# Seven more second exponential parts on VectorE, later passes for them, and feed-forward tiles issued ahead of due passes at one step in four

## The chip, the cores and the metric

The kernel runs on one core of one Trainium2 chip. The metric is the time of one execution on the device in microseconds (us), the median of several runs. The profiler's record of one execution gives every instruction's start and duration.

## The reference, cut to what matters

One transformer block over 2048 tokens with 512 features: layer norm, attention with 32 heads of 16 features, residual; layer norm, a gated feed-forward layer of width 1792, residual.

```python
scores = einsum("bhqd,bhkd->bhqk", q, k) * (Dh ** -0.5)     # 32 heads, 2048 x 2048
p = softmax(scores, axis=-1)
o = einsum("bhqk,bhkd->bhqd", p, v)
h = x + o_as_rows @ wo
g, u = ln(h) @ w_gate, ln(h) @ w_up                          # 512 -> 1792
out = h + (sigmoid(g) * u) @ w_down                          # 1792 -> 512
```

There are 32 x 2048 x 2048 exponentials, 1,048,576 on each of 128 partitions.

## The kernel before, in words

**Steps and cycles.** The exponentials are cut into units of 128 keys x 512 (head, query) columns. Three units make a *step*; there are 683 steps (0 to 682). Four steps make a *cycle*; "place 0" to "place 3" is the step's number modulo 4. A cycle is named here by its first step. In each step `emit_scores` writes the score matmuls of three units (L951) into one of two PSUM tiles `pss` (step number modulo 2), and ScalarE takes the exponential of all three in one instruction (L964, 128x1536). So the scores of step i+2 need the reads of step i's tile to be over.

**Parts on VectorE.** In the steps of the set `split`, ScalarE takes only two units (128x1024) and VectorE computes the third one's exponential by bit arithmetic: `exp_bits` (L989, reads PSUM) at once, and then three *passes*, `exp_first` (L992 and L995) one step later, `exp_second` (L998) two steps later and `exp_third` (L1002, writes the unit) three steps later. They are put into a table of due calls, `due`, by `later`. Place 0 of every cycle from step 8 to 672 has such a part (484 and 540 excepted). Some cycles have a second part at place 2; these steps form the set `twice`. There are 15 from two loops (226, 242, 258, 274, ..., 402, 418, 434, 458, 470) and three given by number (522, 638, 646). In the cycles of `twice` all scores are written as pairs of half-height matmuls, and otherwise those of odd steps only.

**PV.** The product with V (`emit_pv`, L1056) of a cycle's twelve units is three calls, planned by `plan_pv`. All three stand at step n+6 for the cycle that starts at n, those that begin a new group of heads one step later. The accumulator `acc` is one PSUM bank, which `emit_norm` copies out (L1020) at a group's end. The third call reads the unit of a second part: the unit of step n+2 computed on VectorE is the first one of it.

**Filler.** Everything else is a generator, `filler`, that is drawn on step by step through `emit_fill`. From step 185 on it is the output projection and the feed-forward layer of the chunk of queries before the one at work. There are eight chunks: 512, 512, 256, 256 and four of 128 queries. Chunk by chunk it gives the output projection (`ffn_wo` for chunks 0 and 1, `ffn_wo_tight` for the rest: matmuls L650, then addition L662, statistics L149 and the scaling L160 on VectorE, and transposes L166), gate and up (`ffn_up`), and down (`down_tile`, L706 and L711). In `ffn_up` a gate tile (matmuls L687, then tanh on ScalarE, L693) is written at place 3 and an up tile (matmuls L687, then the multiplication on VectorE, L703) at place 1. All these tiles share one PSUM bank, `pm`, so the next tile's matmuls wait until the last one is read. In `ffn_wo` the first half of a projection tile is at place 3 and the second half, with L662 and L149, at place 1. `state["rate"]` is 8.0 while such a chunk's work is issued and None otherwise.

**Order.** Every engine's instructions are issued in the order in which the program calls them. In each step that order is: scores, exponential and bits of step i; PV; the due passes; the filler. Before the change the filler went ahead of the due passes only for a tile that ends in a transpose or a last down part (`state["turn"]`), and ahead of a PV call that begins a new group:

```python
            us = pv_due.pop(i, [])
            early_fill = i >= 2 * CYC and any(u[2] == 0 for u in us)
            for u in us:
                if early_fill and u[2] == 0:
                    emit_fill(i)
                emit_pv(*u[:3], i)
            if state["turn"] and i == state["wait"] and not early_fill:
                emit_fill(i)
                early_fill = True
            for fn in due.pop(i, []):
                fn()
            if 1 <= i < NS and not early_fill:
                emit_fill(i)
```

Of the kernel before, what the change touches and what calls it, by code (L numbers as in the profile page):

```python
# [20 lines left out]
def kernel(  # L21
# [28 lines left out]
    CYC = 4  # L50
# [460 lines left out]
    def first_step(c):  # L511
        return NS * CHUNKS[c][0] / S if c < NC else NS
# [400 lines left out]
    def calm(i):  # L913
        filled = rate(i) and state["wait"] <= i and not state["done"]
        return not filled and not n_pv.get(i, 0)

    def emit_scores(i):
        group = groups[i]
        n = len(group)
        pss = pss2[i % 2]  # L920
        idle = i >= 3 * FIRST and (state["done"] or state["wait"] > i + CYC)
        pairs = i < FIRST and (i < 35 or i % CYC in (1, 2)) or i >= FIRST and (i % 2 == 1 or i - i % CYC + 2 in twice) and not idle
        still = i and calm(i) and calm(i + 1) and i - 1 not in split
        pairs = pairs and not still
        made[i] += 2 if pairs else 3
        if i % CYC == 0 and made[i - 1] <= 3 and i - 1 not in split and not pairs:
            g, s, _, _, j0, _ = part_of(group[0][0], *group[0][2:])
            m = per_bank(group[0][1])
            nc.tensor.matmul(pss[:, 0, :], lhsT=KT[:, g, 0:P], rhs=q_cols(group[0][0], s, j0 if m == 1 else 0, m),
                             start=True, stop=True)  # L930
            made[i] += 1
        order = [(ui, qg, part_of(qg, k, j)) for ui, (qg, c, k, j) in enumerate(group)]
        if pairs and order[0][2][4] // 2 == order[1][2][4] // 2:
            order[1:] = order[:0:-1]
        parts = [u + (a,) for a in range(2) for u in order[:2]] + [u + (a,) for u in order[2:] for a in range(2)]
        if i < OB:
            for ui, (_, c, k, j) in enumerate(group):
                nc.tensor.matmul(pss[:, ui, :], lhsT=KT[:, 0, k * P:(k + 1) * P], rhs=QB[1][:, j, :],
                                 start=True, stop=False)
            for ui, (_, c, k, j) in enumerate(group):  # L940
                nc.tensor.matmul(pss[:, ui, :], lhsT=ident_bf[:, j:j + 1].to_broadcast([P, P]), rhs=bnd[:],
                                 start=False, stop=True)
            parts = []
        for ui, qg, (g, s, kt, nk, j0, nh), a in parts:
            if a >= nk:
                continue
            assert ("k", g // 2) in ready
            h0 = 64 * (j0 // 2)
            rows = slice(h0, h0 + 64) if pairs else slice(0, P)
            o = QC // nk  # L950
            nc.tensor.matmul(pss[:, ui, a * o:(a + 1) * o], lhsT=KT[rows, g, (kt + a) * P:(kt + a + 1) * P],  # L951
                             rhs=q_cols(qg, s, j0, nh, rows), start=True, stop=True,
                             tile_position=(h0, 0) if pairs else None)
        for qg, c, k, j in group:
            if j == 3 and qg + 1 < len(qgs):
                k0 = 12 if per_bank(c) == 1 else 0
                if k == k0:
                    emit_q_rows(qg + 1)
                if k == k0 + (2 if k0 == 0 else 0):
                    emit_q_bound(qg + 1)  # L960
        slot = i % 7
        pt = pt4[slot] if slot < 4 else (pt_early if i < GM else pt_late)[slot - 4]
        na = n - 1 if i in split else n
        ex = nc.scalar.activation(out=pt[:, 0:na, :], in_=pss[:, 0:na, :], func=ACT.Exp, scale=DH ** -0.5 / QS)  # L964
        if na < n:
            scratch = scratch_of(i)
            src, dst = pss[:, na, :], pt[:, na, :]
            if len(scratch[0].shape) == 3:
                src, dst = (v.rearrange("p (a b) -> p a b", a=4) for v in (src, dst))
            tc.declare_no_dep(exp_bits(src, *scratch).ins, ex.ins,  # L970
                              reason="both only read, from different banks")
            later(i + 1, lambda: exp_first(*scratch))
            later(i + 2, lambda: exp_second(*scratch))
            later(i + 3, lambda: exp_third(dst, *scratch))
        for ui, u in enumerate(group):
            p_of[u] = pt[:, ui, :]

# [13 lines left out]
    def exp_first(e_bits, e_man, e_pol):  # L991
        nc.vector.tensor_scalar(out=e_man, in0=e_bits, scalar1=0x7FFFFF, scalar2=-0x40800000,  # L992
                                op0=ALU.bitwise_and, op1=ALU.bitwise_or)
        m = e_man.bitcast(FP32)
        nc.vector.scalar_tensor_tensor(out=e_pol, in0=m, scalar=PA, in1=m, op0=ALU.add, op1=ALU.mult)  # L995

    def exp_second(e_bits, e_man, e_pol):
        nc.vector.scalar_tensor_tensor(out=e_pol, in0=e_pol, scalar=PB, in1=e_man.bitcast(FP32),  # L998
                                       op0=ALU.add, op1=ALU.mult)

    def exp_third(dst, e_bits, e_man, e_pol):
        nc.vector.scalar_tensor_tensor(out=dst, in0=e_pol, scalar=PC, in1=e_bits.bitcast(FP32),  # L1002
                                       op0=ALU.add, op1=ALU.mult)
# [61 lines left out]
    def later(i, fn):  # L1065
        due.setdefault(i, []).append(fn)
# [3 lines left out]
    state = {"turn": False, "wait": 0, "debt": 0.0, "done": False, "next": 0, "rate": None}  # L1070
# [51 lines left out]
    twice = set()  # L1122
    for n0, n1 in ((223, 357), (393, 476)):
        for n in range(n0, n1):
            if n % ((4 if n < n0 + 56 else 3) * CYC) == 0 and n != 448:
                twice.add(n + 2)
    twice |= {522, 638, 646}
    split |= twice
    split -= {484, 540}

    def plan_pv():
        plan, last = {}, 0
        for n, group in enumerate(groups):
            if n < G1:
                if n % CYC == 0:
                    last = n + CYC + 2
                    for k, u in enumerate(units[n * GU:(n + CYC) * GU:4]):
                        if k and u[2] == 0:
                            last += 1
                        plan.setdefault(last, []).append(u)  # L1140
            else:
                for u in group:
                    if u[3] == 3:
                        last = max(last, n + LAG)
                        plan.setdefault(last, []).append(u)
        return plan

    with tc.manual_schedule():
        p1ctx = ExitStack()
        pmh["pool"] = p1ctx.enter_context(tc.tile_pool(name="ps_p1", bufs=6, space=PSUM))  # L1150
        prologue(p1ctx.enter_context(tc.tile_pool(name="pro", bufs=1)))
        p1ctx.close()
        pmh["pool"] = ps_misc
        sctx = ExitStack()
        ps_s = sctx.enter_context(tc.tile_pool(name="ps_s", bufs=1, space=PSUM))
        ptp = sctx.enter_context(tc.tile_pool(name="ptp", bufs=1))
        pss2 = [ps_s.tile([P, GU, QC], FP32, name=f"pss{k}") for k in range(2)]
        pt4 = [ptp.tile([P, GU, QC], BF16, name=f"pt{k}") for k in range(4)]
        later(12, clear_wo)
        later(72, load_wo)  # L1160
        later(90, lambda: nc.gpsimd.tensor_copy(out=ident_f[:], in_=ident_bf[:]))
        load_w()
        pv_due = plan_pv()
        n_pv = {i: len(us) if i < G1 + CYC else 0 for i, us in pv_due.items()}
        for i in range(NS + LAG):
            if i < NS:
                emit_scores(i)
            if i == NS + LAG - 1:
                while next(fl, None) == 1:
                    pass  # L1170
# [3 lines that stand above are left out]
                if early_fill and u[2] == 0:  # L1174
                    emit_fill(i)
                emit_pv(*u[:3], i)
            if state["turn"] and i == state["wait"] and not early_fill:
                emit_fill(i)
                early_fill = True
            for fn in due.pop(i, []):  # L1180
# [3 lines that stand above are left out]
        for _ in fl:  # L1184
            pass
        sctx.close()
        pmh["pool"] = ctx.enter_context(tc.tile_pool(name="ps_t", bufs=6, space=PSUM))
        pmh["work"] = ctx.enter_context(tc.tile_pool(name="tail", bufs=4))
        assert not due
        ffn_last(NC - 1)  # L1190
# [30 lines left out]
```

## Time and profile before

| | |
|---|---|
| median of 3 runs | 938.57 us (938.12 to 938.9) |
| profiled execution: its time, its span | 937.02 us, 935.2 us |
| granted TensorE clock in it | 1.000 |
| exponentials on ScalarE | first 28.6 us, last ends 915.0 us after the span's start |
| busy: ScalarE (ACT), TensorE matmul (PE), VectorE (DVE) | 896.8, 843.0, 760.6 us |
| gate and up multiplications (L703, width 512) | 54 |
| parts on VectorE (bits, L989) | 183 |

Durations are those of one profiled execution. A row of the timeline gives start, duration, engine, line, operation, tiles written and read, count, and in brackets the engine's idle time ahead of it with what ended it. Starts of instructions that follow each other on an engine can lie closer together than the duration of one, since the end of one overlaps with the start of the next. Times are from the span's start.

### The profile page before, as it was taken

To read this page: it belongs to the slowest core of one execution; us is meant where nothing else is said; L and a number is where in the kernel's file an instruction comes from. 1 tells how busy PE (TensorE), PEld (TensorE's weight loads), DVE (VectorE), ACT (ScalarE), POOL (GpSimd) and SP (SyncE) were. 2 spreads that over 40 slices of the span, in tenths; PEclk is the share of its full clock that TensorE was granted. 3 is DMA by queue.
4 is the path that set the end of the run, shared out by engine and by line. 5 is a ranking of instruction groups with operands and counts; after the bars stand their busy time and mean duration, and the time that the engine had idled before them with its cause. 6 is when DMAs were issued, how large, how long until landed. Compare 5 with 4: busy or idle time off the path is not lost.

```text
span 935.2 us, 21055 instructions
## 1 busy us (share of the span) xinstructions
PE 843.0 (90%) x8328; PEld 370.9 (40%) x8328; DVE 760.6 (81%) x1400; ACT 896.8 (96%) x778; POOL 32.5 (3%) x52
## 2 busy tenths in 40 slices
PE   5998888888889999998889999999999999998897
PEld 2322222222223232222233333333555675766575
DVE  8589988888788888898888888888778777778853
ACT  6999999999999999999999999999999999999992
POOL 5300000000000000000000000000000000000000
PEclk9999999999999999999999999999999999999999
DMA  5202350000003000001001100001000101100000
GB/s 165 47 2 68 118 131 16 16 16 11 10 24 106 16 16 16 7 21 28 15 22 27 32 10 16 16 26 33 16 12 26 23 11 22 27 24 17 18 24 14
DMA packets 43599, 29.48 MB, mean 32 GB/s; under 512 B 22764, under 2 KB 39852, under 8 KB 43500
## 3 DMA queue, kind: packets, MB, share of 16 engines
q1 hardware_dynamic: 43356, 28.01, 11.6%
q8 instruction: 65, 1.06, 0.5%
q14 instruction: 34, 0.28, 0.1%
q10 hardware_dynamic: 144, 0.13, 0.0%
HBM read 20.05 MB, written 2.36 MB: 24 GB/s over the span
## 4 chain that ended last, share of the span: by engine, by line
PE 46%; ACT 31%; DVE 15%; issue 5%; DMA 1%; POOL 0%; SPq 0%; ACTq 0%; DVEq 0%; POOLq 0%
PE pss L951 23%; ACT pt L964 17%; PE acc L1056 8%; PE pm L687 6%; ACT stg L964 6%; ACT wd L964 4%; ACT QTu L964 3%; PE pm L706 2%; DVE stg L989 2%; PE pm L650 2%; DVE st L149 1%; PE pm L175 1%; DVE pt L1002 1%; DVE reg L992 1%; DVE y L998 1%
## 5 line engine op out<-in xcount | busy, mean ns | idle before, releaser
L951 PE MATMUL pss<-QB,KT 128*128 128x512 bf16 (+3 forms) x2554 | 476.7, 337 | 54.5 <-ACT pt L964 25.0
L964 ACT ACTIVATE pt<-pss 128x1536 bf16<-128x1536 f32 (+1 forms) x392 | 504.9, 1382 | 7.9 <-PE pss L951 4.1
L951 PEld LDWEIGHTS <-KT 64*128 64x128 bf16 (+1 forms) x2554 | 180.0, 95 | 299.5 <-issue 188.8
L964 ACT ACTIVATE stg<-pss 128x1536 bf16<-128x1536 f32 (+1 forms) x140 | 185.1, 1381 | 3.2 <-PE pss L951 2.1
L989 DVE TENSOR_SCALAR stg<-pss 128x512 int32<-128x512 f32 x120 | 82.8, 690 | 73.6 <-PE pss L951 65.5
L1056 PE MATMUL acc<-pt,Vaug 128*17 128x128 bf16 (+2 forms) x2354 | 108.5, 273 | 3.9 <-DVE xs_all L1020 2.3
L1056 PEld LDWEIGHTS <-Vaug 128*17 128x17 bf16 x4096 | 68.7, 90 | 90.7 <-issue 79.9
L964 ACT ACTIVATE wd<-pss 128x1536 bf16<-128x1536 f32 (+1 forms) x80 | 103.7, 1385 | 0.2
L964 ACT ACTIVATE QTu<-pss 128x1024 bf16<-128x1024 f32 (+1 forms) x71 | 98.0, 1380 | 0.7 <-PE pss L951 0.6
L995 DVE SCALAR_TENSOR_TENSOR y<-reg 128x512 f32<-128x512 f32 x120 | 83.1, 693 | 4.1
L998 DVE SCALAR_TENSOR_TENSOR y<-y,reg 128x512 f32<-128x512 f32 x120 | 82.1, 684 | 1.0
L687 PE MATMUL pm<-reg,reg 128*128 128x128 bf16 (+2 forms) x448 | 58.9, 274 | 3.7 <-DVE reg L703 3.6
L687 PE MATMUL pm<-reg,wu 128*128 128x128 bf16 (+2 forms) x448 | 59.0, 274 | 0.0
L706 PE MATMUL pm<-wd,reg 128*128 128x512 bf16 x210 | 57.9, 382 | 0.0
L992 DVE TENSOR_SCALAR reg<-stg 128x512 int32<-128x512 int32 x120 | 50.5, 421 | 1.8
L693 ACT ACTIVATE sg<-pm 128x512 f32<-128x512 f32 (+1 forms) x58 | 39.1, 674 | 10.1 <-PE pm L687 10.0
L1002 DVE SCALAR_TENSOR_TENSOR pt<-y,stg 128x512 bf16<-128x512 f32 x68 | 46.6, 686 | 1.5
L989 DVE TENSOR_SCALAR wd<-pss 128x512 int32<-128x512 f32 x45 | 31.0, 689 | 18.8 <-PE pss L951 17.6
L1056 PE MATMUL acc<-stg,Vaug 128*17 128x128 bf16 (+2 forms) x998 | 45.7, 257 | 0.4 <-DVE xs_all L1020 0.4
L687 PEld LDWEIGHTS <-reg 128*128 128x128 bf16 x448 | 31.6, 98 | 30.1 <-issue 22.4
L703 DVE SCALAR_TENSOR_TENSOR reg<-sg,pm 128x512 bf16<-128x512 f32 (+1 forms) x58 | 38.6, 665 | 5.1 <-PE pm L687 4.8
L156 POOL TENSOR_TENSOR rs<-ve,pw_neg 128x1 f32<-128x1 f32 x16 | 11.4, 714 | 872.6 <-DVE ve L154 652.8
(155 smaller groups left out, 715.8 us busy)
## 6 DMA issues: line engine op xcount, KB each, us to landing
rb_all<-rd SPq DMA_DIRECT2D x64, 64.0 KB
rb_all<-rd SPq DMA_DIRECT2D x124, 32.0 KB
xr<-in_A_x_dram SPq DMA_DIRECT2D x16, 128.0 KB
QB<-QTu SPq DMA_DIRECT2D x128, 8.0 KB
out_dram<-ob SPq DMA_DIRECT2D x15, 128.0 KB
reg<-in_A_x_dram SPq DMA_DIRECT2D x7, 256.0 KB
KT<-stg SPq DMA_DIRECT2D x7, 256.0 KB
reg<-in_B_w_gate_dram SPq DMA_DIRECT2D x4, 448.0 KB
```

The source lines that it names most:

```text
L687: nc.tensor.matmul(ps[:, i * w:(i + 1) * w], lhsT=wt[:, k, f * P:(f + 1) * P], rhs=hnT[:, k, cols_of(c)], start=(k == 0), stop=(k == DC - 1))
L693: nc.scalar.activation(out=sg[:, 0:n], in_=ps[:, 0:n], func=ACT.Tanh, scale=0.5)
L703: nc.vector.scalar_tensor_tensor(out=out, in0=a, scalar=1.0, in1=b, op0=ALU.add, op1=ALU.mult)
L706: nc.tensor.matmul(ps[:], lhsT=hT[:, f, s * P:(s + 1) * P], rhs=wd[:, f, :], start=(f == 0), stop=(f == FC - 1))
L951: nc.tensor.matmul(pss[:, ui, a * o:(a + 1) * o], lhsT=KT[rows, g, (kt + a) * P:(kt + a + 1) * P], rhs=q_cols(qg, s, j0, nh, rows), start= ...
L964: ex = nc.scalar.activation(out=pt[:, 0:na, :], in_=pss[:, 0:na, :], func=ACT.Exp, scale=DH ** -0.5 / QS)
L989: return nc.vector.tensor_scalar(out=e_bits, in0=src, scalar1=ONE_BITS, scalar2=0.0, op0=ALU.add, op1=ALU.max)
L992: nc.vector.tensor_scalar(out=e_man, in0=e_bits, scalar1=0x7FFFFF, scalar2=-0x40800000, op0=ALU.bitwise_and, op1=ALU.bitwise_or)
L995: nc.vector.scalar_tensor_tensor(out=e_pol, in0=m, scalar=PA, in1=m, op0=ALU.add, op1=ALU.mult)
L998: nc.vector.scalar_tensor_tensor(out=e_pol, in0=e_pol, scalar=PB, in1=e_man.bitcast(FP32), op0=ALU.add, op1=ALU.mult)
L1002: nc.vector.scalar_tensor_tensor(out=dst, in0=e_pol, scalar=PC, in1=e_bits.bitcast(FP32), op0=ALU.add, op1=ALU.mult)
L1056: nc.tensor.matmul(acc[32 * j:32 * j + VW, s * w:(s + 1) * w], lhsT=Vaug[:, kt + a, 4 * g + j, :], rhs=p[:, o:o + w], start=(kt + a == 0), ...
```

## The change

Three things change.

1. Seven steps, the set `slower` (498, 510, 554, 566, 602, 630, 670, all at place 2), join `twice` and `split`: their third unit goes to VectorE.
2. For these seven the three passes come one step later each: first at i+2, second at i+3, third at i+4. `plan_pv` puts the third PV call of such a cycle at step n+7 in place of n+6.
3. At place 1 of every cycle from step 189 on in which `state["rate"]` is set, the filler is issued ahead of the due passes.

```diff
-            later(i + 1, lambda: exp_first(*scratch))
-            later(i + 2, lambda: exp_second(*scratch))
-            later(i + 3, lambda: exp_third(dst, *scratch))
+            slow = int(i in slower)
+            later(i + 1 + slow, lambda: exp_first(*scratch))
+            later(i + 2 + slow, lambda: exp_second(*scratch))
+            later(i + 3 + slow, lambda: exp_third(dst, *scratch))
...
-    twice |= {522, 638, 646}
+    slower = {498, 510, 554, 566, 602, 630, 670}
+    twice |= slower | {522, 638, 646}
...
-                        if k and u[2] == 0:
+                        if k and u[2] == 0 or k == 2 and n + 2 in slower and last == n + CYC + 2:
                             last += 1
...
-            if state["turn"] and i == state["wait"] and not early_fill:
+            ahead = state["rate"] and i % CYC == 1 and i > first_step(1) + 15
+            if (state["turn"] and i == state["wait"] or ahead) and not early_fill:
                 emit_fill(i)
                 early_fill = True
```

In such a cycle, with n its first step, the order on VectorE becomes: bits(n); up(n+1); first(n); bits(n+2); second(n); third(n); bits(n+4); first(n+2); up(n+5); second(n+2); first(n+4); third(n+2); second(n+4); third(n+4).

## The prediction

> **What bounds the kernel now.** I read the page's totals first, then the groups by shape, the busy times by stretch, and last the VectorE and TensorE timelines of single cycles (four steps; step n mod 4 is written "place 0" to "place 3"). I call VectorE's passes over one exponential part *bits* (L989), *first* (L992 and L995), *second* (L998) and *third* (L1002); *up* is L703.
>
> Page totals, then the groups by shape (count, then busy us and mean ns):
>
> ```profile
> PE 843.0 (90%) x8328; PEld 370.9 (40%) x8328; DVE 760.6 (81%) x1400; ACT 896.8 (96%) x778; POOL 32.5 (3%) x52
> L964 ACT ACTIVATE pt<-pss 128x1536 bf16<-128x1536 f32 x285 | 406.9, 1496 | 5.1 <-PE pss L951 1.6 <-PE pss L941 1.3 <-DVE stg L989 0.5
> L964 ACT ACTIVATE pt<-pss 128x1024 bf16<-128x1024 f32 x107 | 115.4, 1079 | 2.8 <-PE pss L951 2.5
> ```
>
> ScalarE sets the pace. A part taken off it saves 1496-1079 = 417 ns by the rows; starts in the timeline lie 1.33 us apart for a full exponential and 0.90 for a cut one, so 0.43 us. Busy time by stretch (an output-projection stretch, then two of gate and up):
>
> ```profile
> 265.00:302.00 37.00, 33.43 (x218) 11.29 (x217) 31.84 (x61) 36.48 (x30) 3.56 (x4) 1.00 0.23 67
> 308.00:382.00 74.00, 69.86 (x442) 21.99 (x443) 63.39 (x108) 73.33 (x69) 0.00 (x0) 1.00 0.06 15
> 655.00:697.00 42.00, 40.46 (x457) 23.17 (x457) 31.24 (x57) 42.00 (x39) 0.00 (x0) 1.00 0.07 14
> ```
>
> The columns are length, PE, PEld, DVE, ACT. From 655 to 697 ScalarE is busy all 42.00 us and VectorE 31.24: a quarter of VectorE looks free. Where it is free, the timeline of cycle 496 shows (it gets a new second part, at step 498):
>
> ```profile
> 665.01 0.69 DVE L989 TENSOR_SCALAR stg<-pss 128x512 int32<-128x512 f32 x1 [0.72 <-PE pss L951]
> 665.48 1.05 PE L687 MATMUL pm<-reg,wu 128*128 128x256 bf16 x8
> 665.74 0.43 DVE L992 TENSOR_SCALAR reg<-stg 128x512 int32<-128x512 int32 x1
> 666.20 0.69 DVE L995 SCALAR_TENSOR_TENSOR y<-reg 128x512 f32<-128x512 f32 x1
> 666.81 0.68 DVE L703 SCALAR_TENSOR_TENSOR reg<-sg,pm 128x512 bf16<-128x512 f32 x1
> 670.19 0.69 DVE L989 TENSOR_SCALAR stg<-pss 128x512 int32<-128x512 f32 x1 [1.37 <-PE pss L951]
> ```
>
> The up matmuls end at about 666.52, 0.82 us after bits ended (665.70). The first pass (665.74 to 666.89) fills that wait exactly. VectorE is then free only at the end of the cycle, 1.37 us before the next bits. Over the up tiles outside the backlogged cycles, the matmul ends 0.72 to 1.20 us after bits; up starts 0.11 us after the matmul at the earliest.
>
> **The change, part by part.** It saves on ScalarE 7 x 0.43 = 3.0 us. It adds to VectorE, for each new part, 0.69+0.43+0.69+0.69+0.69 = 3.19 us.
>
> *Up tiles ahead.* At place 1 the tile work is now issued before the due passes. On VectorE the first pass then queues behind up, and up waits for TensorE, so the wait that the first pass filled becomes idle: 0.8 to 1.2 us per cycle, and what follows is that much later.
>
> In an ordinary gate and up cycle this costs nothing. The idle time before the next bits (0.66 to 1.6 us) covers it. Where cover is short (0.45 to 0.5 us) bits comes up to 0.74 us later, but only scores two steps on wait for it, and they stand behind the next up matmuls, some 1 us, anyway. TensorE's own order is unchanged by this edit.
>
> In a cycle that already had a second part there is no such cover. Cycle 240, VectorE alone:
>
> ```profile
> 334.45 0.69 DVE L989 TENSOR_SCALAR stg<-pss 128x512 int32<-128x512 f32 x1 [0.45 <-PE pss L951]
> ...
> 336.29 0.69 DVE L703 SCALAR_TENSOR_TENSOR reg<-sg,pm 128x512 bf16<-128x512 f32 x1
> 336.90 0.68 DVE L989 TENSOR_SCALAR OT<-pss 128x512 int32<-128x512 f32 x1
> ...
> 341.20 0.69 DVE L1002 SCALAR_TENSOR_TENSOR stg<-OT 128x512 bf16<-128x512 f32 x1
> ...
> 342.87 0.68 DVE L703 SCALAR_TENSOR_TENSOR reg<-sg,pm 128x512 bf16<-128x512 f32 x1
> ```
>
> It runs without a gap. After the change up(241) stays at 336.29, the first pass follows it, and bits(242) moves from 336.90 to 337.97. Up(245) goes ahead of third(242): 1.07+0.61 us later less 0.1 of overlap puts the third from 341.20 to about 342.8, ending 343.5. The PV of step 246 needs that part and stands on TensorE ahead of scores(247), which started at 342.53. PV's last four matmuls take 0.33, so scores start at about 343.85; exponentials start 0.69 after their scores where they wait (step 231: 320.97 to 321.66), so exp(247) starts at 344.5 instead of 343.49. About +0.95 us; less the 0.08 that the late up(245) cost before, +0.87. The same walk gives +0.84 for cycle 224 (its gate's wait of 0.36 us goes, the PV's wait takes its place) and +0.9 for 256. Six such cycles (224, 240, 256, 400, 416, 432) at 0.85 are 5.1 us. Cycle 272, the last up tile, has scores(278) already waiting for bits(276) (0.24 us): +0.9. Cycle 636: +0.4. Sum **+6.4**, bounds 0 to +9.
>
> *Output projection too.* The condition asks for place 1 in the whole feed-forward part, not for up tiles. In chunks 0 and 1 the second half of each projection tile, with its addition (L662) and statistics (L149), is at place 1: eight tiles. Cycle 188:
>
> ```profile
> 266.40 0.69 DVE L989 TENSOR_SCALAR stg<-pss 128x512 int32<-128x512 f32 x1 [1.16 <-PE pss L951]
> ...
> 268.22 0.69 DVE L662 TENSOR_TENSOR reg<-pm,xr 128x512 f32<-128x512 f32 x1
> ...
> 271.29 0.54 DVE L160 TENSOR_SCALAR xn<-reg,mv,rs 128x512 bf16<-128x512 f32 x1
> 271.74 0.68 DVE L989 TENSOR_SCALAR stg<-pss 128x512 int32<-128x512 f32 x1
> ```
>
> The projection matmuls end at 268.18, so L662 can't come earlier, and VectorE idles from 267.09 to 268.29. All behind it is 1.2 us later, bits(192) included: it ends at 273.66 instead of 272.42. Scores(194) wait for it, 273.7 instead of 272.69, and exp(194) starts 0.7 late. The other three tiles of chunk 0 come to 0.4, 0.8 and 0.7. I take 0.6: 8 x 0.6 = **+4.8**, bounds 0 to +7. In later chunks the projection's VectorE work is at places 0 and 3, and the down parts at place 1 end in matmuls alone: nothing.
>
> *The seven new parts.* Starts on VectorE lie 0.61 apart (0.46 behind L992, 0.72 where the next reads the last). Cycle 496 in the new order: bits(496) 665.01; up(497) 666.63; first(496) 667.24; bits(498) 668.31; second and third(496) 668.92 and 669.64; bits(500) 670.25; first(498) 670.86, held back by one step so that bits(500) goes first; up(501) 671.93; second(498) 672.54; first(500) 673.15; third(498) 674.22, ending 674.91. PV's third part, moved to step 503, stands on TensorE behind scores(503), which are done by 673.2, and ahead of gate(503). It waits until 674.97, takes 0.33, and the gate's matmuls bring the tanh (L693) 1.06 later (step 231: gate 322.30, tanh 323.36): 676.36. ScalarE, with its 0.43 saved, would be there at 674.94. So 1.42 late, and exp(504) starts at 676.84, against 675.93 before: a loss of 0.9, saving included. Cycle 564 walks to the same. I take 0.85: 7 x 0.85 = **+6.0**. Bounds per part: -0.43 (no wait) to +1.1.
>
> The row here is VectorE's spare 0.66 to 1.6 us per cycle against 3.19 us added. The Trainium skill (Perfetto Trace Analysis, Optimizing Scalar/DVE Operations) says that where VectorE is saturated, work may better go to ScalarE; this change goes the other way. By that rule the 3.0 us would not be had; with VectorE's mean of 81% in mind they would.
>
> The dearer order of later passes, taken alone: third(498) sits behind first(500) and up(501), which it did not under the earlier order, and gains one step of deadline.
>
> **Sum.** 6.4+4.8+6.0 = 17.2 us, saving included. The profiled execution took 937.02 us (span 935.2 and 1.8 around it), 1.55 below the median of the three runs. 937.02+17.2 = 954.2; on the median, 938.57+17.2 = **955.8**.
>
> **Rivals.** *Faster.* Today's loss around second parts is the late up: up(230) starts 2.28 us after its matmul ended, and ScalarE waits 0.36 us for gate(231). Up ahead ends that. Cycles 228, 260 and 420 last 6.05, 5.82 and 5.83 us against 5.37 of their kind, 1.6 in all; if the thirds come in time, these and the 3.0 us are had: 934.0. It decides at one place: third(498) must end by 673.5 rather than 674.9, that is, the idle time before up must not arise. Against it: up starts 0.11 us behind its matmul in 19 of 53 tiles already, with the first pass ahead of it; without that it can only wait. Chance 0.12.
>
> *New parts alone cost.* Slack in TensorE's queue swallows the moves in the old cycles and the projection; the 6.0 remains: 944.6, with its spread 940.6 to 946. For it: bits may be late by some 0.5 us in ordinary cycles unseen. Against it: the cycles concerned have scores waiting for bits today. Chance 0.12.
>
> *No change*, saving and waits cancelling: 0.03. *Backlog spreads*, each new part delaying the following cycle too, 7 x 0.9 more: 962. Chance 0.05, as the next cycle's VectorE has 0.7 us and more spare.
>
> **How the numbers follow.** The forecast, 946 to 962, has 0.68. The range 941 to 962 takes in the second rival and leaves out 0.20. Within 0.2% (1.9 us, about what a measurement of this kernel can tell from no change): 0.03. Slower by more: 0.85; faster: 0.12.
>
> **What would show it.** Right: up at place 1 with idle time of 0.8 to 1.2 us before it put down to L687, in nearly every gate and up cycle, and less before bits; L1056 waiting for L1002 up to 1.8 us in the new cycles and tanh waiting for L687; L951 or L929 waiting for L989 in the projection cycles. ScalarE's busy time falls by about 3 us, its idle time in the middle grows by about 20. Wrong: no idle time ahead of up, or thirds in time for PV; then the first rival holds.

## The result, and the profile after

| | before | after |
|---|---|---|
| median | 938.35 us (937.14 to 938.9) | 961.4 us (961.17 to 962.89) |
| profiled execution: time, span | 937.02, 935.2 us | 961.27, 959.5 us |
| mean granted TensorE clock in it | 1.000 | 0.995 |
| last exponential ends | 915.0 us | 939.2 us |

The changed kernel is slower by a factor of 1.0258 (95% interval 1.0246 to 1.0271), some 23 us. The forecast was 17.2 us slower, range 941 to 962 on 938.57; the measured ratio lies just above that range (962/938.57 = 1.0250).

Lines of the code have moved by one: bits is now L990, first L993 and L996, second L999, third L1003, PV L1057; up is still L703. The page's totals first, then VectorE's group of up multiplications, ahead of the change and after it (idle time is the number behind the second bar):

```profile
PE 841.4 (88%) x8244; PEld 368.9 (38%) x8328; DVE 779.3 (81%) x1435; ACT 897.4 (94%) x778; POOL 31.2 (3%) x52
```

```profile
L703 DVE SCALAR_TENSOR_TENSOR reg<-sg,pm 128x512 bf16<-128x512 f32 (+1 forms) x58 | 38.6, 665 | 5.1 <-PE pm L687 4.8
```

```profile
L703 DVE SCALAR_TENSOR_TENSOR reg<-sg,pm 128x512 bf16<-128x512 f32 (+1 forms) x58 | 38.7, 668 | 42.1 <-PE pm L687 41.6 <-ACT QTu L964 0.4
```

VectorE's idle time ahead of up has grown from 5.1 to 42.1 us, as forecast. ScalarE's busy time did not fall by the 3 us named: its rows overlap where they follow closely (1496 ns long, 1.33 us apart), and less where it waits, so its losses are read from the starts here. The timeline of cycle 496, VectorE with the PV call that waits for it, and the tanh and the exponential of step 504 behind that ("..." stands for rows left out):

```profile
677.96 0.69 DVE L990 TENSOR_SCALAR stg<-pss 128x512 int32<-128x512 f32 x1
679.64 0.69 DVE L703 SCALAR_TENSOR_TENSOR reg<-sg,pm 128x512 bf16<-128x512 f32 x1 [0.99 <-PE pm L687]
...
681.30 0.68 DVE L990 TENSOR_SCALAR OT<-pss 128x512 int32<-128x512 f32 x1
...
683.42 0.69 DVE L990 TENSOR_SCALAR stg<-pss 128x512 int32<-128x512 f32 x1
684.03 0.42 DVE L993 TENSOR_SCALAR OT<-OT 128x512 int32<-128x512 int32 x1
...
685.09 0.68 DVE L703 SCALAR_TENSOR_TENSOR reg<-sg,pm 128x512 bf16<-128x512 f32 x1
...
687.42 0.68 DVE L1003 SCALAR_TENSOR_TENSOR pt<-OT,OT 128x512 bf16<-128x512 f32 x1
688.16 0.40 PE L1057 MATMUL acc<-pt,Vaug 128*17 128x256 bf16 x8 [1.85 <-DVE pt L1003]
...
689.57 0.60 ACT L693 ACTIVATE sg<-pm 128x512 f32<-128x512 f32 x1 [1.21 <-PE pm L687]
690.56 1.02 ACT L964 ACTIVATE pt<-pss 128x1024 bf16<-128x1024 f32 x1 [0.39 <-PE pss L951]
```

The walk of the prediction put third(498) 9.21 us behind bits(496); it came 9.46 us behind. The tanh was put 11.35 us behind it and came 11.61; exp(504) was put 0.48 us behind the tanh and came 0.99, as it also waited 0.39 us for its scores. Cycle 240, with an old second part:

```profile
338.23 0.69 DVE L990 TENSOR_SCALAR stg<-pss 128x512 int32<-128x512 f32 x1
...
339.85 0.69 DVE L703 SCALAR_TENSOR_TENSOR reg<-sg,pm 128x512 bf16<-128x512 f32 x1 [0.93 <-PE pm L687]
...
345.71 0.68 DVE L703 SCALAR_TENSOR_TENSOR reg<-sg,pm 128x512 bf16<-128x512 f32 x1
346.31 0.68 DVE L1003 SCALAR_TENSOR_TENSOR stg<-OT 128x512 bf16<-128x512 f32 x1
```

Up now leads third(242), which comes 8.08 us behind bits(240) instead of 6.75. And the first projection tile, cycle 188:

```profile
266.41 0.69 DVE L990 TENSOR_SCALAR stg<-pss 128x512 int32<-128x512 f32 x1 [1.16 <-PE pss L951]
268.23 0.69 DVE L662 TENSOR_TENSOR reg<-pm,xr 128x512 f32<-128x512 f32 x1 [1.13 <-PE pm L650]
...
272.94 0.68 DVE L990 TENSOR_SCALAR stg<-pss 128x512 int32<-128x512 f32 x1
```

Bits(192) ends at 273.62; the prediction said 273.66. What it had not foreseen is in the busy times of three neighbouring stretches of 3.4 us (columns: length, PE, PEld, DVE, ACT, POOL, granted clock, DMA share, GB/s):

```profile
699.90:703.30 3.40, 3.40 (x44) 2.41 (x41) 3.23 (x6) 3.40 (x5) 0.00 (x0) 1.00 0.06 10
703.30:706.70 3.40, 1.56 (x27) 1.02 (x20) 3.37 (x9) 2.75 (x3) 0.00 (x0) 1.00 0.07 18
706.70:710.10 3.40, 3.40 (x19) 1.89 (x18) 1.32 (x3) 1.71 (x3) 0.00 (x0) 0.50 0.07 23
```

In the second stretch TensorE stands idle for 1.84 us, held up by the PV call of step 515. In the third, its clock is granted at half speed, and ScalarE is busy for only half of it. The clock falls in the same way from 891.0 and from 928.6 us on (ScalarE busy 2.42 and 2.39 of 3.40 us). The fall at 928.6 follows the PV call of step 675, which waited 1.76 us. The one at 891.0 follows another wait, that of scores(650) for bits(648), which is shorter in the kernel before. Before and after:

```profile
868.85 0.83 PE L951 MATMUL pss<-QB,KT 128*128 128x256 bf16 x6 [1.11 <-DVE stg L989]
```

```profile
890.18 0.83 PE L951 MATMUL pss<-QB,KT 128*128 128x256 bf16 x6 [1.54 <-DVE stg L990]
```

### The profile page after: what moved, and what is told of

The parts are those of the page before. It is cut to its first block, busy times and chain, and to the rows that moved or that the text cites. A ratio compares the mean times of both kernels' runs of the same rounds, so it can differ in the third digit from the quotient of the medians.

```text
span 959.5 us, 21008 instructions
## 1 busy us (share of the span) xinstructions
PE 841.4 (88%) x8244; PEld 368.9 (38%) x8328; DVE 779.3 (81%) x1435; ACT 897.4 (94%) x778; POOL 31.2 (3%) x52
## 4 chain that ended last, share of the span: by engine, by line
PE 43%; ACT 25%; DVE 24%; issue 5%; DMA 1%; POOL 0%; SPq 0%; ACTq 0%; DVEq 0%; POOLq 0%
PE pss L951 22%; ACT pt L964 14%; PE acc L1057 8%; PE pm L687 6%; ACT stg L964 5%; ACT wd L964 4%; PE pm L650 2%; DVE y L996 2%; PE pm L706 2%; ACT QTu L964 2%; DVE stg L990 2%; DVE y L999 2%; DVE reg L703 2%; DVE pt L1003 2%; DVE reg L993 2%
## 5 line engine op out<-in xcount | busy, mean ns | idle before, releaser
L951 PE MATMUL pss<-QB,KT 64*128 64x512 bf16 (+3 forms) x2535 | 472.9, 338 | 59.1 <-ACT pt L964 24.1
L951 PEld LDWEIGHTS <-KT 64*128 64x128 bf16 (+1 forms) x2554 | 175.6, 96 | 307.4 <-issue 187.8
L1057 PE MATMUL acc<-pt,Vaug 128*17 128x128 bf16 (+2 forms) x2354 | 110.0, 275 | 11.9 <-DVE pt L1003 7.2
L990 DVE TENSOR_SCALAR stg<-pss 128x512 int32<-128x512 f32 x120 | 82.8, 690 | 42.4 <-PE pss L951 36.7
L1057 PEld LDWEIGHTS <-Vaug 128*17 128x17 bf16 x4096 | 69.7, 90 | 107.1 <-issue 96.5
L964 ACT ACTIVATE QTu<-pss 128x1024 bf16<-128x1024 f32 (+1 forms) x71 | 95.7, 1347 | 3.0 <-PE pss L951 2.8
L996 DVE SCALAR_TENSOR_TENSOR y<-reg 128x512 f32<-128x512 f32 x120 | 83.1, 692 | 4.1
L999 DVE SCALAR_TENSOR_TENSOR y<-y,reg 128x512 f32<-128x512 f32 x120 | 82.3, 685 | 2.0
L703 DVE SCALAR_TENSOR_TENSOR reg<-sg,pm 128x512 bf16<-128x512 f32 (+1 forms) x58 | 38.7, 668 | 42.1 <-PE pm L687 41.6
L706 PE MATMUL pm<-wd,reg 128*128 128x512 bf16 x187 | 54.4, 381 | 2.6 <-issue 2.1
L993 DVE TENSOR_SCALAR reg<-stg 128x512 int32<-128x512 int32 x120 | 49.7, 414 | 0.4
L1057 PE MATMUL acc<-stg,Vaug 128*17 128x128 bf16 (+2 forms) x998 | 46.1, 256 | 3.7 <-DVE stg L1003 2.6
L693 ACT ACTIVATE sg<-pm 128x512 f32<-128x512 f32 (+1 forms) x58 | 36.0, 620 | 14.0 <-PE pm L687 14.0
L1003 DVE SCALAR_TENSOR_TENSOR pt<-y,stg 128x512 bf16<-128x512 f32 x68 | 46.6, 685 | 1.4
L990 DVE TENSOR_SCALAR wd<-pss 128x512 int32<-128x512 f32 x45 | 31.0, 689 | 18.8 <-PE pss L951 18.1
L687 PEld LDWEIGHTS <-wu 128*128 128x128 bf16 x448 | 31.6, 99 | 25.9 <-issue 18.2
```

The source lines that it names most:

```text
L687: nc.tensor.matmul(ps[:, i * w:(i + 1) * w], lhsT=wt[:, k, f * P:(f + 1) * P], rhs=hnT[:, k, cols_of(c)], start=(k == 0), stop=(k == DC - 1))
L693: nc.scalar.activation(out=sg[:, 0:n], in_=ps[:, 0:n], func=ACT.Tanh, scale=0.5)
L703: nc.vector.scalar_tensor_tensor(out=out, in0=a, scalar=1.0, in1=b, op0=ALU.add, op1=ALU.mult)
L706: nc.tensor.matmul(ps[:], lhsT=hT[:, f, s * P:(s + 1) * P], rhs=wd[:, f, :], start=(f == 0), stop=(f == FC - 1))
L990: return nc.vector.tensor_scalar(out=e_bits, in0=src, scalar1=ONE_BITS, scalar2=0.0, op0=ALU.add, op1=ALU.max)
L1057: nc.tensor.matmul(acc[32 * j:32 * j + VW, s * w:(s + 1) * w], lhsT=Vaug[:, kt + a, 4 * g + j, :], rhs=p[:, o:o + w], start=(kt + a == 0), ...
```

## The experiments

Medians are compared with the kernel before on the same chip (937.14 us in the first four experiments, 937.33 in the next four, 937.21 in the last two).

**Tiles ahead alone** (the kernel before with the third edit of the change):

```diff
-            if state["turn"] and i == state["wait"] and not early_fill:
+            ahead = state["rate"] and i % CYC == 1 and i > first_step(1) + 15
+            if (state["turn"] and i == state["wait"] or ahead) and not early_fill:
```

> The kernel before with the third edit alone: at place 1 the filler goes ahead of the due passes; no new parts, no later passes. Theory (VectorE idles 0.8 to 1.2 us ahead of each up or projection tile, and only the old second-part cycles and the eight projection tiles can't absorb it): about 6.5 us slower from the projection tiles and 6.7 from the old second parts, 13 us in all, some 951.5, with no loss in ordinary gate and up cycles; the granted clock stays 1.000, since no cycle holds a TensorE wait of 1.8 us. Rival (the later passes are what costs, the tiles ahead help or cost little): within 5 us of before.

Measured: 951.24 us, ratio 1.0150 (1.0136 to 1.0164). The clock did not stay at 1.000 in all runs, as had been expected: it did in the profiled one (950.09 us), and the three others, 950.94 to 952.07 us, had 0.998. From the starts of the exponentials in the profiled one, cycle by cycle: the eight projection tiles cost 6.4 us (2.6 in chunk 0, 3.7 in chunk 1), the old second parts 6.7, ordinary gate and up cycles nothing. The theory holds, and its 13 us at a clock of 1.000.

**New parts with later passes, tiles in the old order** (the change without its third edit).

> The changed kernel without its third edit: seven new parts with later passes and the later PV call, tiles in the old order. Theory (the third pass of a new part ends too late because bits of the next cycle, the next first pass and up stand ahead of it, with or without the idle time ahead of up): each new part still loses about 0.9 us net, 5 to 8 us slower than before in all, and the stretches without new parts are as before; the granted clock may still fall once or twice, at 1 to 1.7 us each. Rival (the idle time ahead of up alone makes the thirds late): the seven parts gain up to 3.0 us, some 935.5.

Measured: 942.79 us, ratio 1.0062 (1.0049 to 1.0076). Its runs show the clock as well: 942.35, 942.41 and 942.79 us with 1.000 granted, 944.20 with 0.998, 944.96 with 0.996. The new parts with later passes are dear without tiles ahead, too. In cycle 496 of this kernel:

```profile
670.02 0.69 DVE L990 TENSOR_SCALAR stg<-pss 128x512 int32<-128x512 f32 x1 [0.78 <-PE pss L951]
670.63 0.42 DVE L993 TENSOR_SCALAR OT<-OT 128x512 int32<-128x512 int32 x1
...
673.48 0.68 DVE L703 SCALAR_TENSOR_TENSOR reg<-sg,pm 128x512 bf16<-128x512 f32 x1
674.08 0.68 DVE L1003 SCALAR_TENSOR_TENSOR pt<-OT,OT 128x512 bf16<-128x512 f32 x1
...
674.82 0.40 PE L1057 MATMUL acc<-pt,Vaug 128*17 128x256 bf16 x8 [1.51 <-DVE pt L1003]
```

VectorE now idles 0.78 us ahead of bits(500), with first(498) queued behind it and its input long there, and PV still waits 1.51 us. The order of the passes, with the PV call that goes with it, is a loss in itself; the next experiment gives the comparison.

**New parts alone, old passes, old order:**

```diff
-    twice |= {522, 638, 646}
+    twice |= {498, 510, 554, 566, 602, 630, 670} | {522, 638, 646}
```

> The kernel before with the seven new second parts alone, with the passes and PV of the old second parts, no tiles ahead. Theory: the third pass ends before PV needs it, the next up is some 1.2 us later than now, the gate behind it makes the tanh 0.2 us late: a gain of 0.43 less 0.2 for each, 1 to 2 us faster, about 937. Rival (VectorE has no room for 3.19 us more in these cycles in any order): slower by 3 us and more.

Measured: 936.89 us, ratio 0.9998 (0.9990 to 1.0007): no change, less than the 1 to 2 us expected and far from the rival's 3 us loss. Against the experiment before, at a clock of 1.000 in both (942.41 and 936.62 us, medians of those runs), later passes and the later PV call cost 5.8 us. In cycles 496 and 508 each part saves 0.22 and 0.36 us, and the next cycle gives back 0.29 and 0.26: the gate's matmuls of steps 503 and 515 wait 0.46 and 0.62 us for the late up, and the exponentials behind them are late by about what the part saved.

**New parts, and up between third and first pass.** In a step three steps behind a second part, the filler is drawn when the due list reaches the first pass:

```diff
-            later(i + 1, lambda: exp_first(*scratch))
+
+            def first():
+                exp_first(*scratch)
+            later(i + 1, first)
...
-    twice |= {522, 638, 646}
+    twice |= {498, 510, 554, 566, 602, 630, 670} | {522, 638, 646}
...
             for fn in due.pop(i, []):
+                if state["rate"] and i - 3 in twice and fn.__name__ == "first" and not early_fill:
+                    emit_fill(i)
+                    early_fill = True
                 fn()
```

> The seven new parts alone, old passes and PV, and in the cycle after any second part the up tile is put between the third pass of the second part and the first pass of the next part, a place that costs VectorE no wait because the up matmuls are long done there. Theory: the seven parts gain 0.43 each in full, and the lateness of up behind the old second parts (cycles 228, 260 and 420, 1.6 us in all, and 0.08 in three others) goes: 3 to 4.5 us faster, about 934.5. Rival (another wait takes the place of the late up, such as scores waiting for bits): no better than the seven parts alone.

Measured: 933.87 us, ratio 0.9971 (0.9959 to 0.9982), faster than both kernels. The place is seen in cycle 224 (bits is L992 here, first L995 and L998, third L1005); L1042 and L1045 are the same scaling. Before, and in this version:

```profile
318.58 0.68 DVE L1042 TENSOR_TENSOR OT<-xs_all,rb_all 128x512 bf16<-128x512 f32 x1
...
319.89 0.69 DVE L1002 SCALAR_TENSOR_TENSOR pt<-OT 128x512 bf16<-128x512 f32 x1
...
321.57 0.68 DVE L703 SCALAR_TENSOR_TENSOR reg<-sg,pm 128x512 bf16<-128x512 f32 x1
```

```profile
318.60 0.68 DVE L1045 TENSOR_TENSOR OT<-xs_all,rb_all 128x512 bf16<-128x512 f32 x1
...
319.92 0.69 DVE L1005 SCALAR_TENSOR_TENSOR pt<-OT 128x512 bf16<-128x512 f32 x1
320.53 0.68 DVE L703 SCALAR_TENSOR_TENSOR reg<-sg,pm 128x512 bf16<-128x512 f32 x1
```

Third(226) stays where it was and up comes 1.04 us sooner, without idle time ahead of it. Cycles 228, 260 and 420 are 0.59, 0.45 and 0.46 us shorter, and six of the seven new parts keep 0.2 to 0.3 each.

**The changed kernel with its long TensorE waits kept busy:**

```diff
             for u in us:
...
+                if i - 5 in slower and not early_fill:
+                    spin(pm_tile(), wu[:, 0, 0:QC], 5)
                 emit_pv(*u[:3], i)
...
+            if i == 649:
+                spin(pm_tile(), wu[:, 0, 0:QC], 5)
```

> The changed kernel with five extra matmuls, whose results nobody reads, put on TensorE into each of its long waits: ahead of the moved PV call in steps 503, 515, 607 and 675, and after step 649. They add work and take no wait away. Theory (the part of the loss that the prediction had not counted comes from the granted clock, which falls to half for 3.4 us after a stretch in which TensorE stood idle for 1.5 us and more): the clock stays 1.000 up to the end and the kernel is about 4 us faster than the changed one, some 957.5. Rival (the fallen clock costs nothing, as TensorE waits there anyway): 961 or, with the extra matmuls, more.

Measured: 956.69 us, ratio 1.0205 (1.0189 to 1.0220), 4.7 us faster than the changed kernel with 25 matmuls more; 1.000 is granted in all runs, which lie within 0.1 us. The two stretches that answer to the last two above:

```profile
703.30:706.70 3.40, 2.75 (x29) 1.48 (x26) 3.37 (x9) 2.68 (x2) 0.00 (x0) 1.00 0.08 20
706.70:710.10 3.40, 3.40 (x47) 2.52 (x48) 1.91 (x4) 2.79 (x3) 0.00 (x0) 1.00 0.07 21
```

and the same PV call, which comes no sooner (705.85 in the changed kernel):

```profile
703.87 1.25 PE L270 MATMUL pm<-wu,ident_bf 128*128 128x512 bf16 x5
705.78 0.28 PE L1057 MATMUL acc<-QTu,Vaug 128*17 128x256 bf16 x2 [0.65 <-DVE QTu L1003]
```

Exponential starts against the changed kernel differ in three places only: 1.5 us in cycles 512 and 516, 2.1 in 648, 0.85 in 672 and 676. These follow the three falls of the clock.

**The changed kernel without the projection tiles ahead:**

```diff
-            ahead = state["rate"] and i % CYC == 1 and i > first_step(1) + 15
+            ahead = state["rate"] and i % CYC == 1 and not 185 < i < 217 and not 353 < i < 389
```

> The changed kernel, with the tiles of the output projection of chunks 0 and 1 back behind the due passes, and only gate, up and later tiles ahead. Theory: the eight projection tiles account for 0.7 to 0.9 us each, so it is 6.4 us faster than the changed kernel, about 955. Rival (the loss of these cycles comes back elsewhere, as ScalarE only reaches the next wait earlier): less than 3 us faster.

Measured: 952.67 us, 8.7 faster than the changed kernel, ratio to before 1.0163 (1.0147 to 1.0178). Up to cycle 388 the starts show 6.3 us of it, the projection's. The rest goes with the clock again: in this execution it did not fall behind cycles 512, 648 and 672 (and fell once at 930.8 us, in the tail, where 1.6 us are lost).

**Tiles ahead in ordinary cycles alone** (the first experiment, with two more conditions: not the projection's steps, and neither `i + 1` nor `i - 3` in `twice`).

> The kernel before with tiles ahead of due passes in ordinary cycles alone: not in those of the output projection of chunks 0 and 1, and neither in a cycle with a second part nor in the next one. Theory (idle time ahead of up only takes the place of idle time ahead of the next bits): the same time as before, within 0.5 us, though VectorE's idle time ahead of up grows by some 30 us. Rival (an idle VectorE ahead of up costs everywhere): 3 us slower and more.

Measured: 937.52 us, ratio 1.0001 (0.9992 to 1.0011). VectorE's wait for the up matmuls, before and in this kernel (us in total, times, longest):

```profile
DVE reg L703 <- PE pm L687: 4.8, 5, 1.5
```

```profile
DVE reg L703 <- PE pm L687: 40.5, 44, 1.2
```

36 us more of idle time on VectorE cost nothing here, as foretold.

**The changed kernel with the passes and PV of the new parts as the old ones have them:**

```diff
-            slow = int(i in slower)
+            slow = 0
...
-                        if k and u[2] == 0 or k == 2 and n + 2 in slower and last == n + CYC + 2:
+                        if k and u[2] == 0:
```

> The changed kernel with the passes and the PV call of the seven new parts at the old steps; parts and tiles ahead stay. Theory (later passes put bits, a first pass and up ahead of the third; they lose more than the later PV call gives): each new part loses about 0.9 us by itself, as the old second parts do with tiles ahead, the waits on TensorE are shorter and the clock falls less: 2 to 5 us faster than the changed kernel, 957 to 959. Rival (later passes do help once tiles go ahead): 962 and more.

Measured: 956.68 us (954.81 with a clock of 1.000, to 958.35 with 0.995), ratio 1.0204 (1.0186 to 1.0222), 4.7 faster than the changed kernel. At a clock of 1.000 the comparison is 954.81, a single run, with the kept-busy version's 956.69: later passes (with the later PV call) lose 1.9 us with tiles ahead as well. The starts of the exponentials in the seven cycles agree (2.0 us). The rest, 2.8 us, is a clock that falls less.

**Extra matmuls in the best version** (five after step 649, as above), and that version again.

> The version with the seven new parts, old passes and the up tile between third and first pass, and five extra matmuls on TensorE after step 649, whose results nobody reads. Theory (what lifted single runs of that version from 933.8 to 936.7 is the granted clock falling behind the wait of 0.9 us in step 649): the runs lie closer together, their clock stays 1.000, median about 933.5. Rival (the extra matmuls delay the scores behind them): 0.5 us and more slower than without them.

> The version with the seven new parts, old passes and the up tile between third and first pass, once more beside the one with extra matmuls. Theory: as at its first run, 933.9, with single runs up to 3 us higher where the granted clock fell. Rival (its gain was chance): no faster than before.

Measured: 933.96 us (933.52 to 934.32), ratio 0.9963 (0.9950 to 0.9977), with the extra matmuls; 933.91 (933.71 to 935.27), ratio 0.9966 (0.9953 to 0.9978), without. The gain of the version repeats. The extra matmuls neither cost nor gain in the median, and 0.5 us of improvement did not come; single runs reached 934.3 with them and 935.3 without, too few to say that they help.

## Why the prediction was right, and where it was wrong

The profiled spans differ by 24.3 us. Split by the exponentials' starts:

| term | forecast | measured | from |
|---|---|---|---|
| projection tiles ahead | 4.8 | 6.4 | tiles ahead alone |
| old second parts | 6.4 | 6.7 | tiles ahead alone |
| seven new parts, saving included | 6.0 | 6.5 | kept-busy version less tiles ahead alone |
| fall of the clock | 0 | 4.6 | changed kernel less kept-busy version |
| sum | 17.2 | 24.2 | |

**Right: the mechanism and its places.** VectorE idles ahead of up; what follows is some 1 us late; PV holds up the gate; the projection tiles come along with the condition. Ordinary cycles lose nothing, which the experiment on them alone shows. The Trainium skill (Perfetto Trace Analysis, Optimizing Scalar/DVE Operations) says that, where VectorE is saturated, offloading some of its work to ScalarE may make sense. The change lost time with VectorE busy for 81% of the span, and with up between third and first pass the same seven parts fit on VectorE and give a gain, so here the order in its queue decided.

**Wrong: the sum was made at one TensorE clock.** This is the step that failed. The profile before had 1.000 granted, and the sum kept it there without a reason: the prediction foresaw PV waiting up to 1.8 us and gave these waits no price beyond the delay. The clock fell to half three times, at a cost of 4.6 us. Two falls, with 2.4 us, follow such PV calls; the third, with 2.1 us, follows the wait of scores(650) for bits(648), which the prediction does not mention. With these waits kept busy the ratio is 1.0205, inside the forecast range. The clock is the largest miss, 4.6 of 7.0 us; the mis-sized terms below are the other 2.4. Either alone would have left the result inside the range.

The Trainium skill (TensorE: Matmul & The Clock Gate, What's actually happening) describes a free-running window of 3413 ns after which the clock is set, and a fall behind an idle window. The trace agrees on the length (each fall lasts 3413 ns, and the three start 54 and 11 times that apart), but here a window that was idle for about half was enough, and the measurement decides.

**Mis-sized: the projection term.** The four tiles of chunk 0 were walked at 0.7, 0.4, 0.8 and 0.7 and came to 2.6 us in all. For those of chunk 1 the 0.6 was not walked; they cost 1.04, 0.86, 0.80 and 1.04.

**Partly luck: the new parts.** They cost 0.93 each on average in place of 0.85, but they scatter (kept-busy version against tiles ahead alone). The two that were walked, 496 and 564, were both put at 0.9 and cost 1.6 and 0.5 over two cycles. All seven together cost 7.5 there, and some of it comes back in later cycles; 1.6, and the 1.5 of cycle 600, lie outside the bound of 1.1 for one part. In 496 the walk left out that exp(504) waits for its scores.

**Rivals.** The faster one fell: up ahead of all passes can only wait, and PV waited 1.85 us for third(498). Its observation was sound, since the late up was worth 1.5 us in cycles 228, 260 and 420 once it got a place that costs no wait. "New parts alone cost" fell with the first experiment, "no change" with the result. "Backlog spreads" named 962 us, nearly the measured time, by another mechanism: at a clock of 1.000 the new parts cost 6.5 us and not 12, and the cycle after the next shows no further delay. That later passes, with the later PV call, are themselves a loss, which the prediction only remarked, is shown: 5.8 us without tiles ahead, 1.9 us with them. The passes and the PV call were not tried apart.

## What to carry to other kernels

An engine that is free for a quarter of a stretch is free at one place of the cycle; before an instruction that waits for another engine is moved ahead in an in-order queue, look at which work fills its wait now. To hurry it, put it where its input is already there and ahead of work that nobody waits for yet. When a change makes TensorE wait, price the granted clock as well as the wait.

## What the hardware showed that was not expected

The granted clock fell to 0.50 for exactly 3413 ns after windows of that length in which TensorE's matmul rows left 1.76 to 1.86 us idle in the changed kernel, and 1.54 to 1.72 in most other falls. (Some matmul records are missing, in the changed kernel 8244 rows against 8328 weight loads, so such sums can be too large.) Idle time alone does not decide: the window from 686.2 us, with 1.85 us of it, had no fall behind it, and one in the version without projection tiles, with 1.1 us, had. The three falls took 0.85 to 2.1 us each. Five matmuls (1.25 us) put into each wait prevented all three. What exactly the hardware counts was not settled.

The kernel before pays for the clock as well, in some of its executions. Of its 38 runs beside the experiments, 31 had 0.999 or 1.000 granted and took 936.77 to 937.61 us; six had 0.998 and took 938.00 to 938.99; one had 0.996 and took 940.12. So a few tenths of a per cent between runs of one kernel can be the granted clock, and two versions are best compared at the same one.
